# A memory of attention on one core: the segment's update ahead of its reads, the second half of the read and the update's addition a head later

## The chip, the cores and the metric

One Trainium2 chip; the program runs on one of its cores. The time is that of the device in microseconds (us), the median of several executions of the same program, lower is better. Engines are named as in the profile: PE is the matrix engine (PEld its weight loads), DVE the vector engine, ACT the scalar engine, POOL the GpSimd engine, SP the queue that issues the DMAs.

## The reference

A transformer block over 2048 tokens of width 1024, with 32 heads of 32. The first half is an attention that keeps a memory over four segments of 512 tokens, the second a token-mixing MLP. What matters here is the attention's loop over segments:

```python
phi = lambda t: jnp.where(t > 0, t + 1.0, jnp.exp(t))
for s in range(4):
    qs, ks, vs = q[:, :, s], k[:, :, s], v[:, :, s]
    p = softmax(qs @ ks.T * scale + mask)
    a_dot = p @ vs
    pq = phi(qs)
    a_mem = (pq @ M) / (pq @ z + 1e-6)
    outs.append(g * a_mem + (1 - g) * a_dot)
    pk = phi(ks)
    M = M + pk.T @ vs
    z = z + sum(pk)
```

A segment reads the memory (M, z) as the segments before it left it, and adds its own keys and values afterwards. M and z are zero in segment 0, and what segment 3 would add is read by nobody.

## The kernel before

The program has two parts. The attention (with the output projection's first products) fills the first 1045 us or so of the profile, the MLP the rest. The change lies in the attention alone.

**Tiles.** The 32 heads are taken in 8 groups of 4. A step t of the list `its` (32 of them) is one group and one segment: steps 0 to 15 go through the groups with segments 0 and 1, steps 16 to 31 through the groups again with segments 2 and 3. For each step `project(t, piece)` makes keys and values (pieces 0 and 1, 48 matmuls each, tile nps), queries (piece 2, 24 matmuls, tile qps, and the transposed keys, kps), the feature maps pq and pk, and in piece 3 the values' three bf16 parts and the step's work on the memory. For each of its 4 heads h, `maxima` computes scores a first time (sx, sy, sz) for the row maxima on DVE and turns them by a transpose (nmps) every second head; `scores` computes them again with the maxima as an extra row (a), exponentials on ACT, masks and low halves on POOL; `values` multiplies with the values (pv), and after the fourth head turns the result (ops).

**Order of the work.** One round of the main loop is one head: `scores(n)`, `maxima(n + 3)`, `values(n - 2)`, `project(n + 8)`. So the work on the memory of step t is written 8 heads ahead of that step's first scores. The rows of code only set priorities: a scheduler that knows the dependences reorders the instructions of every engine before the program is built. On the chip each engine then works through its own list strictly in order, and an instruction that waits holds up all behind it.

**The memory step** (`memory(t)`, lines 441 to 466). MZ holds M and z of all groups, 132 columns for each. In segments 1 to 3 the read is done in two halves (two of the segment's four tiles of 128 tokens in each): two matmuls pq by MZ into PSUM (rd, line 450), then three DVE instructions: add 1e-6 to the denominators (line 452), invert them (453), multiply (454, into am). In segments 0 to 2 four matmuls pk by v32 into PSUM follow (up, line 460). In segment 0 DVE writes them masked to MZ (462), in segments 1 and 2 to tm (465), which POOL adds to MZ (466). `am` is wanted by `values` of the same step, some six heads later.

**What they share.** rd, up, nmps, ops and two small transposes (mlt) all use the one PSUM bank with the tag "ms" (`bufs=1`): the next of them cannot start before DVE or ACT has read out the one before. v32, k32, pk and pq have one buffer each: the copies of the next step's values by ACT (line 399) wait until up has read v32.

**DVE's other work** on this stretch matters as well: the low halves of the weights that come in raw (line 122, wv and wq), and the reductions of the modulation's rows (line 573, rawm), which wait for a DMA of 512 KB each.

Of the kernel before, what the change touches and what calls it, by code (L numbers as in the profile page):

```python
# [7 lines left out]
F32 = mybir.dt.float32  # L8
# [4 lines left out]
ALU = mybir.AluOpType  # L13
# [5 lines left out]
P = 128  # L19
# [22 lines left out]
def attention_and_mlp(ctx, tc, x, wq, wkv, wo, beta, w1, b1, w2, b2, c, wm_a, wm_b, out):  # L42
    nc = tc.nc
    V, A, G, T, SY = nc.vector, nc.scalar, nc.gpsimd, nc.tensor, nc.sync
# [17 lines left out]
    a = par.__enter__()  # L62
# [9 lines left out]
    def bank(tag, bufs, name):  # L72
        return psum.tile([P, 512], F32, tag=tag, bufs=bufs, name=name)
# [36 lines left out]
    MZ = acst.tile([P, NG, 132], F32, name="MZ")  # L110
    bdg = acst.tile([P, NG, 132], F32, name="bdg")
# [73 lines left out]
    def kv_chunk(w, h, half, k, ps):  # L185
        wt = w["v", k // 2]
        o = 256 * (k % 2)
        n = 6 * k
        for i, j in ((0, 0), (0, 1), (1, 0)):
            for aa in range(2):  # L190
                tt = 2 * half + aa
                T.matmul(ps[:, aa], h[:, j, 128 * tt:128 * tt + 128], wt[:, i, o:o + 256],  # L192
                         start=(n == 0), stop=(n >= 6 * NK - 2), skip_group_check=True)
                n += 1
# [7 lines left out]
    def two_tiles(ps):  # L202
        return ps.rearrange("p (a n) -> p a n", a=2)
# [116 lines left out]
    for i in range(2):  # L320
        ps = bank("s2", 2, f"scps{i}")
# [22 lines left out]
    b = late.__enter__()  # L344
# [17 lines left out]
    its = [(pr, g, 2 * pr + i) for pr in range(2) for g in range(NG) for i in range(2)]  # L362
    NI = len(its)
    st = {}
# [13 lines left out]
    def project(t, piece):  # L378
        pr, g, seg = its[t]
        if piece == 0:  # L380
            st[t] = {}
        w = W[pr, g]
        hp = [hpages[seg, ct] for ct in range(NK)]
        d = st[t]
        if piece in (0, 1):
            if piece == 0:
                d["k32"] = pj.tile([P, 4, 128], F32, tag="k32", bufs=1, name=f"k32_{t}")
                d["v32"] = pj.tile([P, 4, 132], F32, tag="v32", bufs=1, name=f"v32_{t}")
                G.memset(d["v32"][:, :, 128:132], 1.0)
            half = piece  # L390
            k32, v32 = d["k32"], d["v32"]
            if t:
                ps = two_tiles(bank("pj", 2, f"nps{t}_{half}"))
                for k in range(NK):
                    kv_chunk(w, hp[k], half, k, ps)
            else:
                ps = two_tiles(first[half])
            A.copy(k32[:, 2 * half:2 * half + 2], ps[:, :, 0:128])
            A.copy(v32[:, 2 * half:2 * half + 2, 0:128], ps[:, :, 128:256])
        elif piece == 2:  # L400
            k32 = d["k32"]
            d["sg"] = sg = pj.tile([P, 4, L], F32R, tag="sg", bufs=1, name=f"sg{t}")
            ps = bank("pj", 2, f"kps{t}")
            for i in range(4):
                T.transpose(ps[:, 128 * i:128 * i + 128], k32[:, i], ident)
            split(sg[:, 2:4], ps, A, V)
            if t:
                ps = bank("pj", 2, f"qps{t}")
                for k in range(NK):
                    q_chunk(w, hp[k], k, ps)  # L410
            else:
                ps = first[2]
            split(sg[:, 0:2], ps, A, V)
            if seg:
                r = pj.tile([P, L], F32, tag="tmp", bufs=2, name=f"rq{t}")
                A.activation(r, ps, AF.Relu, scale=-1.0)
                A.activation(r, r, AF.Exp, scale=-1.0)
                d["pq"] = pj.tile([P, L], F32, tag="pq", bufs=1, name=f"pq{t}")
                V.scalar_tensor_tensor(d["pq"], ps, 0.0, r, op0=ALU.max, op1=ALU.add)
            if seg < 3:  # L420
                r = pj.tile([P, L], F32, tag="tmp", bufs=2, name=f"rk{t}")
                kf = k32.rearrange("p a n -> p (a n)")
                A.activation(r, kf, AF.Relu, scale=-1.0)
                A.activation(r, r, AF.Exp, scale=-1.0)
                d["pk"] = pj.tile([P, 4, 128], F32, tag="pk", bufs=1, name=f"pk{t}")
                V.scalar_tensor_tensor(d["pk"].rearrange("p a n -> p (a n)"), kf, 0.0, r, op0=ALU.max, op1=ALU.add)
            for h in range(3):
                stack(t, h)
        else:
            stack(t, 3)  # L430
            v = d["v32"][:, :, 0:128].rearrange("p a (h e) -> p a h e", h=4)
            vp = d["vp"] = b.tile([P, 4, 4, NV], BF16, tag="vp", bufs=3, name=f"vp{t}")
            r1 = pj.tile([P, 4, 4, 32], F32, tag="tmp", bufs=2, name=f"r1_{t}")
            G.memset(vp[:, :, :, 0:1], 1.0)
            A.copy(vp[:, :, :, 1:33], v)
            V.tensor_tensor(r1, v, vp[:, :, :, 1:33], op=ALU.subtract)
            A.copy(vp[:, :, :, 33:65], r1)
            V.tensor_tensor(vp[:, :, :, 65:97], r1, vp[:, :, :, 33:65], op=ALU.subtract)
            memory(t)

    def memory(t):
        pr, g, seg = its[t]
        d = st[t]
        d["am"] = am = b.tile([P, 4, 128], F32, tag="am", bufs=3, name=f"am{t}")
        if seg:
            for half in range(2):
                ps = bank("ms", 1, f"rd{t}_{half}")[:, 0:264].rearrange("p (a n) -> p a n", a=2)
                for aa in range(2):
                    i = 2 * half + aa
                    T.matmul(ps[:, aa], d["pq"][:, 128 * i:128 * i + 128], MZ[:, g], start=True, stop=True)  # L450
                rd = b.tile([P, 2, 4], F32, tag="rd", bufs=2, name=f"rdd{t}_{half}")
                V.tensor_scalar_add(rd, ps[:, :, 128:132], 1e-6)
                V.reciprocal(rd, rd)
                V.tensor_tensor(am[:, 2 * half:2 * half + 2].rearrange("p a (h e) -> p a h e", h=4),
                                ps[:, :, 0:128].rearrange("p a (h e) -> p a h e", h=4),
                                rd.unsqueeze(3).to_broadcast([P, 2, 4, 32]), op=ALU.mult)
        if seg < 3:
            ps = bank("ms", 1, f"up{t}")
            for i in range(4):
                T.matmul(ps[:, 0:132], d["pk"][:, i], d["v32"][:, i], start=(i == 0), stop=(i == 3))  # L460
            if seg == 0:
                V.tensor_tensor(MZ[:, g], ps[:, 0:132], bdg[:, g], op=ALU.mult)
            else:
                tm = b.tile([P, 132], F32, tag="tm", bufs=1, name=f"tm{t}")
                V.tensor_tensor(tm, ps[:, 0:132], bdg[:, g], op=ALU.mult)
                G.tensor_tensor(MZ[:, g], MZ[:, g], tm, op=ALU.add)

    def maxima(t, h):
        d = st[t]
# [123 lines left out]
    def at(f, n):  # L593
        if 0 <= n < 4 * NI:
            f(n // 4, n % 4)
# [3 lines left out]
    def seg_load(seg):  # L599
        seg_x[seg] = [load_x(s2p, tt) for tt in range(4 * seg, 4 * seg + 4)]  # L600
        return norm_all(seg_x[seg])
# [9 lines left out]
    with tc.issue_after(last_wm.ins):  # L611
        _, exp, _, normed_v = seg_load(1)
# [58 lines left out]
    for g in range(2, NG):  # L671
        n = 8 * g - 13
# [5 lines left out]
    for j in range(32):  # L678
        n = ML0 + 2 * j + (8 if j >= 8 else 0)
        later(n, lambda j=j: mod_fetch(j), n + (2 if j < 8 else 1), lambda r, j=j: mod_late(j, r), "V")  # L680
    plan(WO0 - 3, lambda: spread(gaw, 0))
    for i in range(8):
        n = WO0 + WOS * i
        later(n, lambda i=i: wo_fetch(i), n + 1, lambda r, i=i: wo_split(i, r), "G")

    for n in range(-LEADS, 4 * NI + VL):
        at(scores, n)
        at(maxima, n + LEADS)
        at(values, n - VL)
        m = n + LEADP  # L690
        if 0 <= m + 4 < 4 * NI:
            t = (m + 4) // 4
            if its[t][:2] not in W:
                with tc.issue_after(last_sk[t - 2 if t > 16 else 0, 3].ins):
                    load_w(its[t][1], its[t][0])
        if m >= 8:
            at(project, m)
        if 59 <= m < 67:
            seg, ct = 2 + (m - 59) // 4, 2 * ((m - 59) % 4)
            with ExitStack() as s:  # L700
                if seg == 3:
                    s.enter_context(tc.issue_after((last_sk[15, 3] if ct < 4 else last_nt[14, 3]).ins))
                reload_h(seg, ct)
                reload_h(seg, ct + 1)
        if 4 * NI - 5 <= m < 4 * NI + 3:
            i = m - 4 * NI + 5
            for c in (2 * (i % 4), 2 * (i % 4) + 1):
                wop[c, i // 4] = new_page(f"wo{c}_{i // 4}")
                if c < 5 or i < 4:
                    SY.dma_start(wop[c, i // 4].bitcast(F32), wos[c, i // 4])  # L710
        for f, engines in todo.pop(n, ()):
            with behind(n, engines):
                f()
# [135 lines left out]
    for products, tt in (((0, 1), 0), ((2,), 1), ((3, 4, 8), 8), ((9,), 9), ((10,), 2), ((11,), 10), ((12,), 3),  # L849
# [5 lines left out]
        for i in products:  # L855
            if i > 1:
                f = product(i)
# [283 lines left out]
```

## Time and profile before

| | |
|---|---|
| median of 3 executions | 2224.89 us (2224.09 to 2230.13) |
| the profiled execution: its own time / its span | 2226.6 us / 2224.9 us |
| PE busy in the span | 2190.3 us, 98% |
| DVE, ACT, POOL busy | 1666.7, 1135.7, 725.8 us |
| matmuls of the memory's reads (rd) / updates (up) | 192 records, 31.3 us / 192 records, 28.0 us |
| transposes of the maxima (nmps) in the same bank | 64 |

The matmuls of 32-bit data with 132 columns appear as two records each, so two rd matmuls are "x4" in a row of the timeline. Busy PE time in the profile contains modelled ends, so that neighbouring matmuls overlap; how many of one kind went through in a stretch of the timeline tells their rate better than the mean of one.

### The profile page before, as it was taken

What the parts mean: (1) busy time and instruction counts of PE and PEld (TensorE: products, weight loads), DVE (VectorE), ACT (ScalarE), POOL (GpSimd) and SP (SyncE); (2) the same over time, 40 slices, a digit from 0 to 9 for tenths busy, and PEclk for the clock granted to TensorE, in tenths of its full rate; (3) what the DMA queues carried; (4) which work ended last, traced back from release to release, by engine and by line L of the source; (5) the groups of instructions that cost most, each with busy time, mean ns of one, the idle gap of its engine ahead of it and who ended that gap; (6) DMA issues with size and microseconds to landing.
All of it is one profiled execution on the core that took longest, in us unless ns stands there. A gap on an engine that the chain in (4) does not pass through costs nothing.

```text
span 2224.9 us, 38052 instructions
## 1 busy us (share of the span) xinstructions
PE 2190.3 (98%) x13786; PEld 1881.0 (85%) x13786; DVE 1666.7 (75%) x3762; ACT 1135.7 (51%) x2050; POOL 725.8 (33%) x831
## 2 busy tenths in 40 slices
PE   8999999999999999999999999999999999999999
PEld 5988898888999999888888888888888888888887
DVE  7676777756777777664858766888888886969687
ACT  5486776756666666654636533533334242424232
POOL 2175766646767776663002200033330000000000
PEclk9999999999999999999999999999999999999999
DMA  7666666686556666664754687655556542414134
GB/s 287 192 187 191 175 181 193 189 279 216 170 180 205 188 183 211 193 219 143 231 194 186 226 304 275 243 223 220 204 202 219 206 148 64 145 57 147 57 123 151
DMA packets 175183, 423.03 MB, mean 190 GB/s; under 512 B 17524, under 2 KB 71828, under 8 KB 166036
## 3 DMA queue, kind: packets, MB, share of 16 engines
q1 hardware_dynamic: 174996, 420.61, 57.5%
q8 instruction: 109, 1.79, 0.3%
q14 instruction: 78, 0.64, 0.1%
HBM read 244.62 MB, written 125.06 MB: 166 GB/s over the span
## 4 chain that ended last, share of the span: by engine, by line
PE 87%; DVE 5%; DMA 3%; ACT 2%; POOL 1%; issue 1%; SPq 0%; DVEq 0%; ACTq 0%
PE mx L921 48%; PE nps L192 11%; PE po L791 8%; PE qps L200 7%; PE pv L544 3%; PE a L515 1%; PE sz L478 1%; PE sx L478 1%; DMA sk<-nt 1%; PE up L460 1%; PE a L518 1%; POOL p L530 1%; PE a L522 1%; PE sy L478 1%; PE rd L450 1%
## 5 line engine op out<-in xcount | busy, mean ns | idle before, releaser
L921 PE MATMUL mx<-bU,sp 128*128 128x512 f32 x2352 | 534.3, 389 | 0.9 <-DVE ac L928 0.9
L921 PEld LDWEIGHTS mx<-bU,sp 128*128 128x128 f32 x2352 | 441.3, 188 | 93.4 <-issue 1.3
L119 ACT CAST sp<-wr 128x384 fp32r<-128x384 f32 (+2 forms) x408 | 218.1, 547 | 431.8 <-PE mx L921 349.1
L192 PE MATMUL nps<-wv,h 128*128 128x256 f32 x3072 | 431.2, 283 | 1.6 <-DVE h L122 0.7
L921 PE MATMUL mx<-bA,sp 128*128 128x512 f32 x1764 | 430.5, 389 | 0.0
L530 POOL TENSOR_TENSOR p<-p,ph 128x640 f16<-128x640 f32 x256 | 380.2, 1485 | 138.5 <-ACT ph L528 134.5
L192 PEld LDWEIGHTS nps<-wv,h 128*128 128x128 f32 x3072 | 400.3, 189 | 9.4 <-DVE h L122 2.0
L921 PEld LDWEIGHTS mx<-bA,sp 128*128 128x128 f32 x1764 | 331.2, 188 | 68.7
L122 DVE TENSOR_TENSOR sp<-wr,sp 128x384 fp32r<-128x384 f32 (+2 forms) x408 | 259.8, 648 | 24.7 <-ACT sp L119 24.4
L928 DVE TENSOR_TENSOR ac<-mx,ac 128x512 f32<-128x512 f32 x280 | 189.9, 687 | 85.2 <-PE mx L921 84.1
L200 PE MATMUL qps<-h,wq 128*128 128x512 f32 x768 | 197.9, 400 | 0.0
L528 ACT CAST ph<-p 128x1280 f16<-128x1280 f32 x128 | 161.4, 1261 | 59.7 <-POOL p L526 59.6
L791 PE MATMUL po<-wo,ots 128*128 128x512 f32 x768 | 180.9, 391 | 0.0
L791 PEld LDWEIGHTS po<-wo,ots 128*128 128x128 f32 x768 | 142.7, 188 | 28.7
L200 PEld LDWEIGHTS qps<-h,wq 128*128 128x128 f32 x768 | 141.6, 190 | 27.7
L921 PE MATMUL mx<-bB,sp 128*128 128x512 f32 x588 | 164.0, 389 | 0.0
L526 POOL TENSOR_SCALAR_AFFINE_SELECT p<-p 128x256 f32<-128x256 f32 x256 | 134.1, 529 | 81.8 <-ACT p L523 53.9
L921 PEld LDWEIGHTS mx<-bB,sp 128*128 128x128 f32 x588 | 110.4, 188 | 22.9
L480 DVE CUSTOM_DVE_ANT_0 sz<-sz,mask 128x512 f32<-128x512 f32 x128 | 89.1, 696 | 52.0 <-PE sz L478 49.5
L480 DVE CUSTOM_DVE_ANT_0 sx<-sx,mask 128x128 f32<-128x128 f32 (+1 forms) x256 | 93.7, 366 | 44.1 <-PE sx L478 37.9
L928 DVE TENSOR_TENSOR cc<-mx,cc 128x512 f32<-128x512 f32 x140 | 94.9, 684 | 37.6 <-PE mx L921 37.4
L516 ACT ACTIVATE p<-a,shift 128x512 f32<-128x512 f32 x128 | 88.4, 691 | 41.2 <-PE a L515 40.4
(209 smaller groups left out, 3244.7 us busy)
## 6 DMA issues: line engine op xcount, KB each, us to landing
sk<-sg SPq DMA_DIRECT2D x384, 128.0 KB
wr<-in_w_dram SPq DMA_DIRECT2D x28, 1024.0 KB
wr<-in_w_dram SPq DMA_DIRECT2D x32, 768.0 KB
bstu<-ucd SPq DMA_DIRECT2D x28, 768.0 KB
wsp<-wv SPq DMA_DIRECT2D x32, 512.0 KB
rawm<-in_wm_b_dram SPq DMA_DIRECT2D x32, 512.0 KB
wv<-wsp SPq DMA_DIRECT2D x32, 512.0 KB
pcd<-cc SPq DMA_DIRECT2D x14, 1024.0 KB
```

The source lines that it names most:

```text
L119: last_hi[0] = A.copy(hi, src)
L122: return lo_eng.tensor_tensor(lo, src, hi.bitcast(F32), op=ALU.subtract)
L192: T.matmul(ps[:, aa], h[:, j, 128 * tt:128 * tt + 128], wt[:, i, o:o + 256], start=(n == 0), stop=(n >= 6 * NK - 2), skip_group_check=True)
L200: T.matmul(ps, wt[:, i, o:o + 128], h[:, j], start=(k + n == 0), stop=(3 * k + n == 3 * NK - 1))
L480: marks[4 * t + h - LEADS, "V"] = V.tensor_tensor_reduce(o, o, mask[:, 384 - 128 * i:], 1.0, -3.0e38, op0=ALU.add, op1=ALU.max, accum_out= ...
L516: A.activation(p32[:, 0:512], b0, AF.Exp, scale=SCALE, bias=shift)
L526: G.affine_select(w, w, pattern=[[0, 2], [1, 128]], compare_op=ALU.is_ge, fill=0.0, base=0, channel_multiplier=-1)
L528: marks[n, "A"] = A.copy(hi, p32)
L530: marks[n, "G"] = G.tensor_tensor(lo[:, c], p32[:, c], hi[:, c], op=ALU.subtract)
L791: T.matmul(ps, os_[:, i, P * ct:P * ct + P], wop[ct, nh][:, j], start=(n == 0), stop=(n == 3 * NK - 1))
L921: T.matmul(ps, ops[q][:, i, P * k:P * k + P], b[:, j], start=(m == 0 and first), stop=(m == 3 * nk - 1), skip_group_check=True)
L928: V.tensor_tensor(d, ps, d, op=ALU.add)
```

## The change

What was one call of `memory(t)` becomes two. Step 0, at the old place, first does the update (the four matmuls and DVE's masked copy), then the first half of the read. Step 1, called a head later in the main loop, behind piece 0 of the next step's `project`, does the second half of the read and POOL's addition of tm to MZ, which has to come behind both halves. In segment 0 nothing but the update is done, and MZ is written at once, as before. The instructions are the same in kind and number on every engine; pools and buffers are the same.

```diff
-            memory(t)
+            memory(t, 0)
...
-    def memory(t):
+    def read(t, half):
         pr, g, seg = its[t]
         d = st[t]
-        d["am"] = am = b.tile([P, 4, 128], F32, tag="am", bufs=3, name=f"am{t}")
-        if seg:
-            for half in range(2):
-                ps = bank("ms", 1, f"rd{t}_{half}")[:, 0:264].rearrange("p (a n) -> p a n", a=2)
...
+        ps = bank("ms", 1, f"rd{t}_{half}")[:, 0:264].rearrange("p (a n) -> p a n", a=2)
+        for aa in range(2):
+            i = 2 * half + aa
+            T.matmul(ps[:, aa], d["pq"][:, 128 * i:128 * i + 128], MZ[:, g], start=True, stop=True)
+        rd = b.tile([P, 2, 4], F32, tag="rd", bufs=2, name=f"rdd{t}_{half}")
+        V.tensor_scalar_add(rd, ps[:, :, 128:132], 1e-6)
+        V.reciprocal(rd, rd)
+        V.tensor_tensor(d["am"][:, 2 * half:2 * half + 2].rearrange("p a (h e) -> p a h e", h=4),
+                        ps[:, :, 0:128].rearrange("p a (h e) -> p a h e", h=4),
+                        rd.unsqueeze(3).to_broadcast([P, 2, 4, 32]), op=ALU.mult)
+
+    def update(t):
+        pr, g, seg = its[t]
+        d = st[t]
+        ps = bank("ms", 1, f"up{t}")
+        for i in range(4):
+            T.matmul(ps[:, 0:132], d["pk"][:, i], d["v32"][:, i], start=(i == 0), stop=(i == 3))
+        if seg == 0:
+            V.tensor_tensor(MZ[:, g], ps[:, 0:132], bdg[:, g], op=ALU.mult)
+        else:
+            d["tm"] = tm = b.tile([P, 132], F32, tag="tm", bufs=1, name=f"tm{t}")
+            V.tensor_tensor(tm, ps[:, 0:132], bdg[:, g], op=ALU.mult)
+
+    def memory(t, step):
+        pr, g, seg = its[t]
+        d = st[t]
+        if step == 0:
+            d["am"] = b.tile([P, 4, 128], F32, tag="am", bufs=3, name=f"am{t}")
+            if seg < 3:
+                update(t)
+            if seg:
+                read(t, 0)
+        elif seg:
+            read(t, 1)
+            if seg < 3:
+                G.tensor_tensor(MZ[:, g], MZ[:, g], d["tm"], op=ALU.add)
...
         if m >= 8:
             at(project, m)
+        if m % 4 == 0 and 0 < m <= 4 * NI:
+            memory(m // 4 - 1, 1)
```

Since the scheduler works on the whole attention, the order of all engines differs from step 1 on. Three places are shown, all of step 13 (group 6, segment 1). The first number in a name is the step: up13 is the update of step 13, rd13_1 the second half of its read, nps14 the next step's projection, nmps12_3 the transposed maxima of step 12; sy, sz and a are scores.

PE before, from the second half of the read to the update (pv matmuls and their weight loads stand where the dots are):

```order
L450 MATMUL rd13_1_6481<-MZ_127,pq13_6383 128x132 x2
...
L192 MATMUL nps14_0_6575<-wv0_7_1_1_6402,h0_7_451 128x256 x6
L192 MATMUL nps14_1_6692<-wv0_7_1_1_6402,h0_6_423 128x256 x5
L192 MATMUL nps14_1_6692<-wv0_7_1_1_6402,h0_7_451 128x256 x6
L478 MATMUL sy_13_1_6765<-sk1_1_502 128x384
L478 MATMUL sz_13_1_6768<-sk1_1_502 128x512
L521 MATMUL a2_12_0_6516<-sk0_0_497 128x128
L522 MATMUL a2_12_0_6516<-sk0_0_497 128x256
L515 MATMUL a0_12_1_6631<-sk0_1_498 128x512
L460 MATMUL up13_6488<-v32_13_6066,pk13_6388 128x132 x4
```

PE with the change, from the update to the first half of the read, and from there to the second half:

```order
L460 MATMUL up13_6474<-v32_13_6066,pk13_6388 128x132 x4
L493 MATMUL sz_13_1_6768<-sk1_1_502 128x512
L530 MATMUL a0_12_0_6502<-sk0_0_497 128x512
L533 MATMUL a1_12_0_6505<-sk0_0_497 128x384
L447 MATMUL rd13_0_6481<-MZ_127,pq13_6383 128x132 x2
...
L192 MATMUL nps14_0_6567<-wv0_7_1_0_6399,h0_4_367 128x256 x4
L192 MATMUL nps14_1_6692<-wv0_7_1_0_6399,h0_4_367 128x256 x4
L501 MATMUL nmps12_3_6528<-ident_90,mx12_2_6425 8x128
...
L493 MATMUL sy_13_2_6881<-sk1_2_503 128x384
L405 MATMUL kps14_6807<-ident_90,k32_14_6564 128x128 x2
L447 MATMUL rd13_1_6618<-MZ_127,pq13_6383 128x132 x2
```

The update stood behind the second half of the read and now stands ahead of the first. Between the two halves there is now a use of the bank by nmps12_3, and 40 nps matmuls lie between that and rd13_1.

DVE at the same place, before, from the end of the first half (am13 from rd13_0) to the end of the second:

```order
L454 TENSOR_TENSOR am13_6473<-rd13_0_6474,rdd13_0_6477 128x256
...
L573 SCALAR_TENSOR_TENSOR rawm5_6406,mcol_529<-rawm5_6406,scb_76 128x1024
L122 TENSOR_TENSOR wq0_7_0_0_6496<-rawq7_0_6279,wq0_7_0_0_6496 128x512
L122 TENSOR_TENSOR wq0_7_0_1_6499<-rawq7_0_6279,wq0_7_0_1_6499 128x512
L452 TENSOR_SCALAR rdd13_1_6484<-rd13_1_6481 128x8
L547 RECIPROCAL pv11_2_6546<-pv11_2_6546 128x4
L453 RECIPROCAL rdd13_1_6484<-rdd13_1_6484 128x8
L549 TENSOR_REDUCE red11_2_6568<-pv11_2_6546 128x128
L454 TENSOR_TENSOR am13_6473<-rd13_1_6481,rdd13_1_6484 128x256
```

and with the change:

```order
L465 TENSOR_TENSOR tm13_6479<-up13_6474,bdg_128 128x132
...
L449 TENSOR_SCALAR rdd13_0_6484<-rd13_0_6481 128x8
L450 RECIPROCAL rdd13_0_6484<-rdd13_0_6484 128x8
L451 TENSOR_TENSOR am13_6473<-rd13_0_6481,rdd13_0_6484 128x256
L122 TENSOR_TENSOR wv0_7_1_0_6399<-rawv7_1_6125,wv0_7_1_0_6399 128x512
L122 TENSOR_TENSOR wv0_7_1_1_6402<-rawv7_1_6125,wv0_7_1_1_6402 128x512
L588 SCALAR_TENSOR_TENSOR rawm5_6406,mcol_529<-rawm5_6406,scb_76 128x1024
L122 TENSOR_TENSOR wq0_7_0_0_6488<-rawq7_0_6279,wq0_7_0_0_6488 128x512
L122 TENSOR_TENSOR wq0_7_0_1_6491<-rawq7_0_6279,wq0_7_0_1_6491 128x512
L504 SCALAR_TENSOR_TENSOR nt1_12_3_6531<-nmps12_3_6528,nt0_12_3_6530 8x128
```

The reduction of rawm5 and the two weight splits behind it (wq) stood between the two halves of the read, on which the update waited. Now the update and the first half are read out ahead of them, the next step's weights (wv) come behind these, and what stands right behind rawm5 and wq is the reading out of nmps12_3.

More of the change, by code (lines that the diff above doesn't have):

```diff
@@ L438, in project @@
             V.tensor_tensor(vp[:, :, :, 65:97], r1, vp[:, :, :, 33:65], op=ALU.subtract)
-            memory(t)
-    def memory(t):
+            memory(t, 0)
+    def read(t, half):
         pr, g, seg = its[t]
         d = st[t]
-        d["am"] = am = b.tile([P, 4, 128], F32, tag="am", bufs=3, name=f"am{t}")
-        if seg:
-            for half in range(2):
-                ps = bank("ms", 1, f"rd{t}_{half}")[:, 0:264].rearrange("p (a n) -> p a n", a=2)
[L448 to L466, printed above, removed]
```

## The prediction

> **What bounds the kernel now.** I read the page first, then the busy time by stages, then what PE waited for in the stage that is changed, and last the timeline round its longest wait. The page, and the two stages:
>
> ```profile
> span 2224.9 us, 38052 instructions
> PE 2190.3 (98%) x13786; PEld 1881.0 (85%) x13786; DVE 1666.7 (75%) x3762; ACT 1135.7 (51%) x2050; POOL 725.8 (33%) x831
> ...
> 57.00:1045.00 988.00, 966.91 (x8348) 878.13 (x8347) 697.20 (x2065) 642.57 (x1146) 614.49 (x719) 0.99 0.65 194
> 1045.00:2225.00 1180.00, 1175.41 (x5183) 972.41 (x5181) 928.62 (x1614) 463.20 (x856) 99.15 (x64) 1.00 0.52 182
> ```
>
> (After the stretch and its length: PE, PEld, DVE, ACT, POOL busy, granted clock, DMA share, GB/s.) PE sets the time in both. The change touches the first stretch alone, in which PE is idle for 988.0 - 966.9 = 21 us of 988. The change leaves the number of matmuls as it is, so it can only alter these 21 us and the clock at which the rest runs. What PE waited for there (total, times, longest):
>
> ```profile
> PE a L515 <- DMA sk<-nt: 4.1, 5, 1.4
> PE up L460 <- DVE am L454: 3.8, 3, 3.5
> PE a L521 <- ACT p L516: 2.4, 3, 1.0
> ...
> PE sy L478 <- DVE rdd L453: 1.1, 1, 1.1
> ...
> PE kps L405 <- ACT v L399: 0.6, 1, 0.6
> ...
> PE nmps L486 <- DVE tm L465: 0.4, 1, 0.4
> ```
>
> The memory's own waits are few, but one of them, 3.5 us of up behind am, is the longest of the stretch. In PE's timeline (start, length, x number of records, idle time before it and what ended it):
>
> ```profile
> 438.63 2.91 PE L192 MATMUL nps<-wv,h 128*128 128x256 f32 x24
> 441.38 0.34 PE L478 MATMUL sy<-sk 96*128 96x384 f32 x1
> 441.56 0.40 PE L515 MATMUL a<-sk 98*128 98x512 f32 x1
> 441.79 0.34 PE L518 MATMUL a<-sk 98*128 98x384 f32 x1
> 441.97 0.62 PE L450 MATMUL rd<-MZ,pq 128*128 128x132 f32 x4
> 442.34 0.48 PE L478 MATMUL sz<-sk 96*128 96x512 f32 x1
> 442.65 0.61 PE L544 MATMUL pv<-vp,ph 128*128 128x97 bf16 x10
> 443.09 1.19 PE L192 MATMUL nps<-wv,h 128*128 128x256 f32 x8
> ...
> 448.13 0.70 PE L450 MATMUL rd<-MZ,pq 128*128 128x132 f32 x4
> ...
> 451.42 0.40 PE L515 MATMUL a<-sk 98*128 98x512 f32 x1
> 455.29 2.10 PE L460 MATMUL up<-v,pk 128*128 128x132 f32 x8 [3.48 <-DVE am L454]
> ```
>
> This is step 13. The second half of the read is issued at 448.13, PE works on until 451.8, and the update then waits 3.48 us for the bank. Why DVE was late, and what the granted clock did (eighth column of the windows):
>
> ```profile
> 449.51 1.92 DVE L573 SCALAR_TENSOR_TENSOR rawm<-rawm,scb 128x1024 f32<-128x1024 f32 x1 [1.55 <-DMA rawm<-in_wm_b_dram]
> ...
> 451.36 2.69 DVE L122 TENSOR_TENSOR wq<-rawq,wq 128x512 fp32r<-128x512 f32 x2
> 453.97 0.15 DVE L452 TENSOR_SCALAR rdd<-rd 128x8 f32<-128x8 f32 x1
> ...
> 454.73 0.41 DVE L454 TENSOR_TENSOR am<-rd,rdd 128x256 f32<-128x256 f32 x1
> ```
>
> ```profile
> 128.00:130.00 2.00, 1.35 (x7) 1.04 (x7) 1.95 (x9) 2.00 (x5) 2.00 (x5) 1.00 1.04 289
> 130.00:132.00 2.00, 1.45 (x8) 0.82 (x6) 1.74 (x6) 2.00 (x5) 0.71 (x3) 1.00 0.98 188
> ...
> 134.00:136.00 2.00, 2.00 (x13) 2.00 (x12) 2.00 (x2) 2.00 (x5) 1.92 (x2) 0.50 0.90 228
> ```
>
> ```profile
> 452.00:454.00 2.00, 0.00 (x0) 0.00 (x0) 2.00 (x3) 1.72 (x4) 1.51 (x2) 0.96 1.02 383
> 454.00:456.00 2.00, 0.71 (x3) 0.74 (x4) 2.00 (x10) 0.00 (x0) 0.52 (x2) 0.50 1.05 332
> ...
> 462.00:464.00 2.00, 2.00 (x6) 1.54 (x5) 2.00 (x8) 0.33 (x3) 1.14 (x2) 0.50 0.84 324
> 464.00:466.00 2.00, 2.00 (x10) 1.65 (x9) 1.69 (x3) 0.55 (x2) 1.96 (x2) 0.98 0.94 277
> ```
>
> DVE, in order, waited 1.55 us for rawm's DMA, reduced it, split two weights, and only then read out rd. PE's pause took the clock to half from 453.9 to 464.1, so the stall costs more than its own length.
>
> **The change part by part.** The sum is made against the profiled execution: its own time 2226.6 us (span 2224.9 and 1.7 round it), 1.7 us above the median of 2224.89.
>
> *The stall of step 13.* Now: 3.48 us idle, then 455.3 to 464.1 = 8.8 us at half clock, in which half as much gets done: 4.4 us more. Together 7.9 us. With the change the update stands ahead of the first half, and nothing waits for the second half's evacuation but the next user of the bank. What stands there instead is priced with these groups (count, then busy total, mean ns):
>
> ```profile
> L122 DVE TENSOR_TENSOR wv<-rawv,wv 128x512 fp32r<-128x512 f32 x27 | 36.0, 1358 | 3.5 <-ACT wv L119 3.5
> L454 DVE TENSOR_TENSOR am<-rd,rdd 128x256 f32<-128x256 f32 x48 | 20.2, 420 | 0.7
> L122 DVE TENSOR_TENSOR wq<-rawq,wq 128x512 fp32r<-128x512 f32 x14 | 18.1, 1306 | 0.4 <-ACT wq L119 0.3
> L489 DVE SCALAR_TENSOR_TENSOR nt<-nmps,nt 8x128 fp32r<-8x128 f32 x64 | 17.5, 274 | 19.5 <-ACT nt L488 19.4
> L453 DVE RECIPROCAL rdd<-rdd 128x8 f32<-128x8 f32 x48 | 9.4, 197 | 0.7
> L452 DVE TENSOR_SCALAR rdd<-rd 128x8 f32<-128x8 f32 x48 | 7.7, 160 | 14.7 <-PE rd L450 14.6
> ```
>
> First, the next step's nps needs the first wv split, which DVE now does behind the first half's evacuation: 0.16 + 0.20 + 0.42 + 1.36 = 2.1 us after rd. Beside it PE has ten pv matmuls (442.65 to 443.09: 0.45 us). That leaves a wait of about 1.6 us. Second, rd13_1 needs the bank that nmps12_3 holds until DVE's nt. DVE needs from the end of rd13_0: 0.8 for the evacuation, 2 x 1.36 (wv), 1.55 (rawm, by its usual length: 49.5 us for 32), 2 x 1.31 (wq), 0.27 (nt) = 8.0 us, and its wait for the DMA. That landed at 449.5, 6.9 us after rd13_0's end; since rd13_0 stands some 2.1 us of PE work later with the change (sz, two a and the four up among others), it lands 4.8 us after its end, DVE asks for it after 3.5, waits 1.3, and nt is done after 9.3 us. PE by then has 0.45 + 1.6 waited + 8 nps (0.9) + 40 nps at (441.38 - 438.63) / 24 = 0.115 us (4.6) + about 1.7 for ten pv, seven score and two kps matmuls at the spacings above = 9.3 us. So some 0.3 us of wait, if any. Left over: 1.9 us, in pieces of under 2 us. Term: **-7.9 + 1.9 = -6.0 us**. If the DMA is 2 us later than before, rd13_1 waits those 2 us as well; if the wv wait finds the score work already done, it is nothing: 0 to 4 us are left over.
>
> The clock could still fall. By the rows at 128 to 132, 1.2 us of idle time spread over 4 us was enough for the half clock at 134 (that spell lasted about 3.4 us by its three windows, 1.7 us lost). So a wait of 1.6 us may cost 1.7 more; this goes into the range, not into the sum.
>
> [...]
>
> *The other waits of the same kind.* The rest of up behind am (3.8 - 3.5 = 0.3 us), nmps behind tm (0.4; up and nmps stood next to each other in step 1), kps behind ACT's copy of v, which waits for up (0.6), and sy behind DVE's work on the denominators (1.1): all come from the two reads and the update following each other through one bank. With up first and the second half a head away they go: **-2.4 us**; bounds 0 and -2.4, and I take all, since in each of the 24 steps the update's own evacuation is one instruction of 0.3 us.
>
> *What is added.* The second half now stands between nmps of the odd heads and the next nmps or ops, in 24 places. Where that bank is tight, a wait of nmps's evacuation (ACT, then DVE's 0.27) or of rd's (0.78) falls on PE. Counting matmuls between two users of the bank at the spacings above, fewer than 2.2 us of PE work lie between them in 16 places with the change, 23 before. Below: nothing. Above: 24 x 0.78 = 18.7 us, if nothing covered them. The nearest rows are the short waits of today's chain, 0.3 + 0.4 us over 24 steps, so I take **+1.0 us**.
>
> POOL's addition of tm (16 instructions) is a head later; its result is read by the next segment's read, four heads or more on. pq is held a head longer, and is written again in the next piece 2, a head after the second half is due. v32, k32 and pk come free earlier. The DMAs are the same and SP is not asked for more. All that costs nothing unless DVE is late by a head, some 8 us.
>
> Sum: -6.0 - 2.4 + 1.0 = **-7.4 us**: 2219.2 for an execution like the profiled one, **2217.5 us** for the median.
>
> **The rivals.**
>
> *The stall moves instead of going.* rawm's DMA, the two wq splits and DVE's strict order are all still there. If the DMA lands 3 us later against PE, rd13_1 or pv catches the same 3.5 us and the half clock with it. For it: DMA is saturated there (shares of 1.02 and 1.05). Against it: the 9.3 us of work that now stand between. Then only the small waits change: 2224.9 - 2.4 + 1.0 = 2223.5 us. A new cold spell anywhere else in the reordered attention gives about the same, 2217.5 + 7.9 = 2225.4.
>
> *Slower: the bank becomes a chain through the maxima.* nmps, then rd's second half, then the next nmps or ops: each waits for DVE's evacuation of the last, and nt feeds the DMA on which the second score pass waits already (4.1 us, 5 times). It decides where DVE needs longer than PE has work in between, about 3.4 us. Then step 13, where DVE is latest, is held up as it is today and keeps its 7.9 us; if half of the 24 second halves lose their 0.78 us, that is 9.4 us, and one more spell at half clock adds 4.4: 2224.9 - 2.4 + 9.4 + 4.4 = 2236 us. For it: the bank has its 170 uses as before, and one of them now waits between two evacuations that feed the maxima. Against it: DVE is busy for 697 of 988 us and has time to catch up.
>
> *Nothing happens,* because the scheduler would put the pieces back where they were: the orders of PE and DVE exclude it.
>
> **How the numbers follow.** 0.3%, 6.7 us, is about what a measurement of this kernel can tell from no change. The forecast has 0.50, and since its -7.4 lies close to that bound and its left-over wait is 0 to 4 us, 0.40 of this is faster and 0.10 the same. The stall that moves has 0.27: 0.22 same, 0.02 faster, 0.03 slower. The slower chain has 0.23: 0.22 slower, 0.01 same. Together: faster 0.42, same 0.33, slower 0.25. The forecast's own range is 2211 to 2222: downward nothing left over, nothing added and the cold spell at 134 gone as well (2217.5 - 1.9 - 1.0 - 1.7 = 2213) and 2 us of the 11 us of other idle time; upward 4 us left over, half of the small waits still there, and 1.7 us of half clock (2217.5 + 2.1 + 1.2 + 1.7). The whole range takes in the stall that moves and reaches almost to the slower case's 2236; below, it allows for half of the idle time that is left of the 21 us: 2208 to 2235.
>
> **What would show it.** In the profile of the changed kernel: up waits for am nowhere; no window near 450 to 465 with a clock of 0.5; PE's idle time between 57 and 1045 falls from 21 to about 13 us, with a wait of 1 to 2 us of nps behind wv in step 13, and rd behind nt at 0.3 us; ACT's copies of v no longer wait for up. Wrong would be the forecast if that stall or a half clock shows at another instruction (the first rival), or if rd behind nt and nmps or ops behind am sum up to 8 us or more (the second).

## The result, and the profile after

| kernel | median of its runs, us | lowest to highest | ratio to before (95% interval) |
| --- | --- | --- | --- |
| before | 2225.33 (6 runs) | 2223.67 to 2230.13 | |
| with the change | 2239.56 (6 runs) | 2237.44 to 2241.12 | 1.0060 (1.0047 to 1.0073) |

The change makes the kernel 14.2 us (0.6%) slower. 2217.5 was forecast, and the range ended at 2235.

The head of the page of the changed kernel, and then its two stages (after the stretch and its length: PE, PEld, DVE, ACT, POOL busy, granted clock, DMA share, GB/s):

```profile
span 2238.5 us, 38027 instructions
PE 2196.8 (98%) x13786; PEld 1884.4 (84%) x13786; DVE 1666.9 (74%) x3762; ACT 1135.1 (51%) x2050; POOL 722.1 (32%) x831
```

```profile
57.00:1045.00 988.00, 962.21 (x8310) 873.14 (x8309) 692.90 (x2060) 642.94 (x1145) 611.01 (x719) 0.99 0.64 193
1045.00:2238.00 1193.00, 1186.22 (x5225) 980.19 (x5223) 933.59 (x1620) 462.71 (x858) 98.96 (x64) 1.00 0.52 181
```

In the attention PE's idle time did not fall from 21 us to 13; it rose to 988.0 - 962.2 = 25.8 us. At the end of that stretch 8348 matmuls were through before, 8310 now, and the rest has to be done later.

From 1045 us on, PE's list is the same in both kernels. The first matmul of this common part starts 9.5 us later with the change, the last one 13.4 us later. So 3.9 us of the loss arise in the second stretch, which the change does not touch. PE's waits after 1150 us, first before, then with the change:

```profile
PE mx L921 <- DVE ac L928: 0.9, 1, 0.9
```

```profile
PE mx L938 <- DVE ac L945: 2.6, 2, 1.7
PE mx L938 <- ACT sp L119: 1.1, 2, 0.7
```

That is 2.8 us more of idle time. Over the kernels of this study the idle time behind 1045 us lies between 0.9 and 3.7 us; whether the 3.7 belong to the change's order or to this one execution is not shown.

**The place that was forecast** looks much as forecast. PE's timeline in step 13 (start, length, instruction, x records, idle time before it and what ended it):

```profile
449.72 0.45 PE L493 MATMUL sy<-sk 96*128 96x384 f32 x1 [0.42 <-DVE mx L495]
...
450.24 1.06 PE L460 MATMUL up<-v,pk 128*128 128x132 f32 x8
451.05 0.48 PE L493 MATMUL sz<-sk 96*128 96x512 f32 x1
452.22 0.47 PE L530 MATMUL a<-sk 98*128 98x512 f32 x1 [0.69 <-ACT ph L543]
...
452.71 0.61 PE L447 MATMUL rd<-MZ,pq 128*128 128x132 f32 x4
...
455.75 0.96 PE L192 MATMUL nps<-wv,h 128*128 128x256 f32 x6 [0.87 <-DVE wv L122]
```

The update runs ahead of the read and waits for nothing, where it had waited 3.48 us. The spell at half clock (granted 0.50) from 453.8 to 464.1 is gone. The wait of nps for the wv split is there, 0.87 us where 1.6 was forecast.

**What took its place** stands elsewhere. What PE waited for in the attention now (total, times, longest):

```profile
PE nps L192 <- DVE sg L122: 2.6, 1, 2.6
PE a L536 <- ACT p L531: 2.6, 4, 1.2
PE a L530 <- DMA sk<-nt: 2.4, 4, 1.4
PE nps L192 <- DVE wv L122: 2.0, 3, 0.9
PE nps L192 <- ACT wv L119: 1.9, 2, 1.3
PE pv L559 <- DVE red L566: 1.9, 3, 1.0
PE sx L493 <- DMA sk<-sg: 1.9, 2, 1.7
PE sz L493 <- DVE mx L495: 1.5, 3, 1.0
...
PE up L460 <- DVE pk L426: 1.3, 1, 1.3
PE kps L405 <- ACT k L398: 1.1, 1, 1.1
...
PE rd L447 <- DVE tm L465: 0.7, 1, 0.7
```

Most of them do not belong to the memory: they are projections waiting for weights or for the step before, and scores and values waiting for maxima, exponentials and transposed maxima. The memory's own are up behind pk, which is the very first update (at 60 us) and waited 1.3 us before the change too, and the last row. And the half clock (0.50) stands at three places where it did not stand before, from 334.0, 433.0 and 497.8 us on. The second, in windows of two us:

```profile
428.00:430.00 2.00, 0.63 (x17) 0.51 (x14) 2.00 (x4) 1.83 (x3) 1.89 (x2) 1.00 0.00 0
430.00:432.00 2.00, 1.34 (x5) 0.71 (x5) 1.93 (x7) 1.41 (x3) 2.00 (x2) 1.00 0.00 0
432.00:434.00 2.00, 0.88 (x3) 0.48 (x3) 2.00 (x10) 1.48 (x2) 0.63 (x3) 0.75 0.89 186
434.00:436.00 2.00, 1.65 (x9) 1.45 (x10) 1.74 (x4) 2.00 (x5) 1.92 (x2) 0.50 0.92 197
```

PE was idle for 3.15 of the 6 us from 428 to 434, in short pieces, with DVE at work for 5.9 us of that time. The clock fell to 0.50 at 433.0, when 2.2 us of this had gone by. The third place is the longest wait of the stretch; the timelines of PE, ACT and SP's queue there, and the windows behind it:

```profile
498.45 2.93 PE L192 MATMUL nps<-wv,h 128*128 128x256 f32 x12 [2.56 <-DVE sg L122]
```

```profile
497.09 0.58 ACT L119 CAST sg<-kps 128x512 fp32r<-128x512 f32 x1 [6.19 <-DMA sk<-nt]
```

```profile
468.80 6.81 SPq L359 DMA_DIRECT2D h<-hT  x8
476.56 0.68 SPq L374 DMA_DIRECT2D sk<-sg  x1
...
492.50 0.58 SPq L376 DMA_DIRECT2D sk<-sg  x1
```

```profile
498.00:500.00 2.00, 1.55 (x7) 1.55 (x8) 2.00 (x8) 1.21 (x3) 0.41 (x1) 0.50 0.38 111
500.00:502.00 2.00, 2.00 (x11) 1.90 (x10) 0.26 (x2) 1.23 (x2) 0.00 (x0) 0.50 1.01 387
502.00:504.00 2.00, 2.00 (x11) 1.90 (x10) 1.93 (x8) 0.00 (x0) 0.00 (x0) 0.50 0.83 248
```

Read backwards: nps waits for DVE's low half of the transposed keys (sg), DVE for ACT's cast, ACT stood 6.2 us waiting for a transfer of sk, and SP's queue sent eight reloads of the activations (h<-hT, 6.8 us) ahead of this step's first sk. A run below holds the reloads back. Nothing of this is part of the memory step; it is where the reordered attention happens to be at that moment.

**The account of the time.** From the traces of all 18 kernels of this study: PE's idle time ahead of matmuls after 57 us, plus what the clock lost (length of each spell times one minus the granted clock), and the rest of the profiled execution's time.

| kernel | profiled, us | idle | lost to the clock | rest |
| --- | --- | --- | --- | --- |
| before | 2226.6 | 22.0 | 6.8 | 2197.8 |
| with the change | 2240.6 | 29.5 | 8.5 | 2202.6 |
| fastest of the study | 2216.6 | 16.3 | 0.0 | 2200.3 |
| slowest of the study | 2242.9 | 33.2 | 6.8 | 2202.9 |
| all 18 | 2216.6 to 2242.9 | 16.3 to 33.2 | 0 to 10.2 | 2196.1 to 2203.6, mean 2200.8 |

So idle time and half clock account for most of what sets these kernels apart: 24 us between the fastest and the slowest of 26. For the change they are 7.5 + 1.7 = 9.2 us of the profiled difference of 14.0; of the 7.5, 4.7 lie in the attention and 2.8 behind it. Some 0.4 us were lost ahead of the 57 us from which the table counts, where the changed kernel has one more spell, of 3.4 us at 50.7 us. For the remaining time the trace shows no wait of PE; it is within the 7.5 us by which the rest scatters over the kernels.

The table has one execution of each kernel, and the spells are not the same in every execution. PE's list is the same in all 18 kernels up to 82 us, and yet three of them have a spell at 50.3 to 50.7 us and fifteen have none. On one chip 21 executions of the kernel before had granted clocks of 0.995 to 0.999 over the whole span; one of 0.995 took 2233.9 us, the one of 0.999 took 2224.3 us. So what an order costs in half clock is partly chance.

### The profile page after: what moved, and what is told of

Same layout as the page of the kernel before. It is cut to its first block, busy times and chain, and to the rows that moved or that the text cites. A ratio compares the mean times of both kernels' runs of the same rounds, so it can differ in the third digit from the quotient of the medians.

```text
span 2238.5 us, 38027 instructions
## 1 busy us (share of the span) xinstructions
PE 2196.8 (98%) x13786; PEld 1884.4 (84%) x13786; DVE 1666.9 (74%) x3762; ACT 1135.1 (51%) x2050; POOL 722.1 (32%) x831
## 4 chain that ended last, share of the span: by engine, by line
PE 87%; DVE 4%; DMA 4%; ACT 2%; POOL 1%; issue 1%; SPq 0%; ACTq 0%; DVEq 0%
PE mx L938 46%; PE nps L192 13%; PE qps L200 7%; PE po L808 7%; PE pv L559 4%; PE a L530 1%; PE sz L493 1%; PE sx L493 1%; POOL p L545 1%; PE a L533 1%; PE sy L493 1%; PE rd L447 1%; PE up L460 1%; PE a L537 1%; DMA sk<-sg 1%
## 5 line engine op out<-in xcount | busy, mean ns | idle before, releaser
L538 ACT ACTIVATE p<-a,shift 128x384 f32<-128x384 f32 x128 | 74.2, 580 | 66.3 <-PE a L537 65.5
```

## The experiments

Four theories run through the expectations. A: the change makes a new order of the whole attention, and that order happens to put other waits and half clock in PE's way. B: the second half, a head late, makes the chain through the one bank longer. C: the update ahead of the read costs. D, formed after the first runs: the two parts of the change cost together. Times in one row come from one chip.

### One part alone, one half of the steps alone

The change has two parts, the update first and the second half a head late. Against the changed kernel:

```diff
+        first, late = True, False     # e1: update first, nothing late
+        # e2: False, True    e3: t >= 16, t >= 16    e4: t < 16, t < 16
...
-            if seg < 3:
+            if first and seg < 3:
                 update(t)
             if seg:
                 read(t, 0)
-        elif seg:
+                if not late:
+                    read(t, 1)
+            if not first and seg < 3:
+                update(t)
+        elif seg and late:
             read(t, 1)
-            if seg < 3:
-                G.tensor_tensor(MZ[:, g], MZ[:, g], d["tm"], op=ALU.add)
+        if seg in (1, 2) and step == late:
+            G.tensor_tensor(MZ[:, g], MZ[:, g], d["tm"], op=ALU.add)
```

> One part of the change alone: the update ahead of the reads, both halves of the read and POOL's addition behind it at the old place. Theory A (the loss of 14.2 us is made by the new order of the whole attention, which puts other waits and half-clock spells in PE's way; the memory step itself costs nothing): the order of every engine is drawn anew here too, so the time is neither that of before nor that of the change but somewhere from 2220 to 2240 us, and the two parts alone do not add up to +14. Theory B (the second half, a head later, lengthens the chain through the bank): the late half is not here, so 2225 us within 3 us. Theory C (the update ahead of the reads costs): 2239 us within 3 us.

> The other part alone: first half of the read, then the update at the old place, second half and addition a head later. Theory A: somewhere from 2220 to 2240 us, its difference from before plus that of the update-first kernel not 14 us. Theory B: 2239 us within 3 us, with rd behind nt, or nmps and ops behind am, as new waits of PE that sum up to 5 us or more. Theory C: 2225 us within 3 us.

> The whole change, but only for steps 16 to 31 (segments 2 and 3); up to some 480 us the program is that of before. Theory A: no share of the loss belongs to it by itself; since the spells at half clock and the waits that were worst in the change lie before 510 us, 2220 to 2230 us. Theory B or C: 16 of the 24 changed reads and 8 of the 16 changed updates are here, so half to two thirds of the loss, 2232 to 2235 us.

> The whole change for steps 0 to 15 alone (segments 0 and 1); up to some 480 us the program is that of the change. Theory A: the attention is 5 to 7 us behind that of before at 510 us, as the change was, and what comes behind is drawn anew, 2228 to 2240 us. Theory B or C: a third to a half of the loss, 2230 to 2232 us, spread evenly over the steps and not at two or three places.

| run | median, us | before on that chip | difference |
| --- | --- | --- | --- |
| e1 update first | 2231.59 | 2227.98 | +3.6 |
| e2 half late | 2215.85 | 2227.98 | -12.1 (ratio 0.9936, 0.9920 to 0.9953) |
| e3 second pass | 2234.01 | 2227.98 | +6.0 |
| e4 first pass | 2235.64 | 2227.98 | +7.7 |

The two halves of the steps add up to the change (13.7 of 14.2). For e3 theory A had expected 2220 to 2230 us and failed, while the 2232 to 2235 of B and C held; for e4 A's range held and theirs failed. The traces show why the sum need not speak against A: up to 543 us PE's list in e4 is that of the change, and from 640 us on PE's list in e3 is that of the change, so each has the change's own order in its half.

The two parts do not add up: 3.6 - 12.1 = -8.5 against +14.2. The late half makes the chain through the bank longer, and is the fastest kernel of the study, below the one before; so that chain (theory B) is not what costs. Its attention:

```profile
57.00:1045.00 988.00, 974.83 (x8413) 887.07 (x8411) 704.69 (x2084) 646.82 (x1154) 613.03 (x719) 1.00 0.65 197
```

Its idle time is 988.0 - 974.8 = 13.2 us, which is what had been forecast for the whole change, and the profiled execution has no spell of half clock in the attention.

### The wait at 498 taken away

```diff
+                if seg == 2:
+                    s.enter_context(tc.issue_after(last_sk[14, 3].ins))
```

The reload of the activations of segment 2 is held until step 14's last sk has been sent.

> The changed kernel, with the reload of segment 2's normed tokens held back until the last head rows of step 14 are issued; up to some 465 us the program is that of the change. In the change SP issues six reloads in a row (469.9 to 475.6 us) ahead of step 14's head rows, ACT then waits 6.2 us for their landing before it may overwrite sg, PE waits 2.6 us at 498 us, and 6.8 us at half clock follow. If that is what this place costs: the wait and the spell at 498 us are gone, 2.6 + 3.4 = 6 us, so the attention is that much less behind at 510 us. Theory A (order of the whole): what follows is drawn anew, so the end is 2 to 10 us under the change. Theory D (the two parts of the change together cost by themselves): no more than the 6 us, and the loss behind 510 us (3 us in the attention) stays as it is.

Measured 2237.55 us, 9.4 us above the kernel before on that chip (2228.1), where the change has 14.2. The wait of nps for sg is gone, and the first rows of PE's waits are now:

```profile
PE a L533 <- DMA sk<-nt: 8.0, 4, 3.5
PE sx L496 <- DMA sk<-sg: 3.4, 3, 1.4
```

The transposed maxima come late instead (8.0 us where the change has 2.4). One wait taken away by a new order of the queue came back as another: the attention's idle time is 26.4 us, where the change has 25.8, and in place of the spell at 497.8 there is one of the same 6.8 us at 521.2.

### The same order drawn anew: token tiles shifted

The token tiles (one DVE job every six heads) have nothing to do with the memory. Put one or two heads later, they make the scheduler reorder nearly the whole attention again (PE's list differs from 89 us on), under each of the memory's versions:

```diff
-        later(6 * i, lambda i=i: load_gaw(i),
-              6 * i + 3, lambda r, i=i: token_tile(8 + i), "V")
+        later(6 * i + 1, lambda i=i: load_gaw(i),
+              6 * i + 4, lambda r, i=i: token_tile(8 + i), "V")
```

(With 2 and 5 for two heads.)

> A control: the kernel before with other work, the normalizing of segment 2's and 3's tokens, written one head later; the memory is untouched, but the order of all engines differs from step 2 on. Theory A: as much of a new draw as the change was, so the time moves by 3 to 15 us either way against before. Theory D: within 3 us of before.

> The same shift on the changed kernel. Theory A: its distance to the control made from before is not the 14 us of the change, but differs from it by 5 us or more. Theory D: 14 us above that control, within 4 us.

> The same shift on the kernel with the second half late and the update at its old place (12 us under before without the shift). Theory A: the gain shrinks or goes, its distance to the control made from before is anywhere from -10 to +10 us. Theory D: 12 us under that control, within 4 us.

> The kernel before with its token tiles two heads later; the memory step is as before. A third draw of the control, after 2228.1 (no shift) and 2233.7 (one head). Theory A (what decides is where the new order of the whole attention happens to let TensorE wait and fall to half clock): somewhere between 2222 and 2240. Theory D (the two parts of the change together cost by themselves): the same, since D says nothing of the control; D speaks of the distances to it in the other three.

> The whole change with the token tiles two heads later. So far it stood 14 us above its control without a shift and 9 us above it with one head of shift. D: again 8 to 14 us above h1. A: the distance to h1 is drawn anew, between -6 and +12 us, and a value under +4 would speak for A.

> The second half of the read and the addition a head later, the update at its old place; token tiles two heads later. So far 12 us and 6.5 us below its control. D: 5 to 12 us below h1. A: between -12 and +6 us of h1; above -2 would speak for A.

> The update ahead of both halves of the read, nothing a head later; token tiles two heads later. Without a shift it stood 3 us above its control. D: 0 to 5 us above h1, since only the two parts together cost. A: anywhere between -6 and +10 us. If h2 and h4 both lie well above h1, and h3 below, it is the update's place ahead of the read that costs, whatever the second half does (theory C).

| shift | control | the change | half late alone | update first alone |
| --- | --- | --- | --- | --- |
| none | 2225.33 / 2227.98 | +14.2 | -12.1 | +3.6 |
| one head | 2233.72 (before 2228.1) | 2242.89, +9.2 | 2227.23, -6.5 | not run |
| two heads | 2229.52 (before 2227.61) | 2236.81, +7.3 | 2224.10, -5.4 | 2235.31, +5.8 |

("Control" is the kernel before with the same shift; the differences are those to it.) A shift that computes nothing new moves the kernel before by 5.6 and by 1.9 us. The first is nearly as large as the gain of 7.4 that was forecast. With one head, theory D's three bounds failed: the control within 3 us, the change 10 to 18 us above it (missed by 0.8), the late half 8 to 16 us below it; A's held, that for the change barely. Yet in three draws of three the change is above its control and the late half alone below it. With two heads D's bounds for the change (8 to 14) and for the update alone (0 to 5) were missed by under 1 us, while the value under +4 that would have spoken for A did not come: this spoke for something systematic. With two heads the change and the update alone lie well above the control and the late half below it; that was the sign, named beforehand, that the update's place ahead of the read costs (theory C). The draws are not quite independent: PE's list in the change with a shift of one head is the same as without it from about 645 us on.

### Is it the read right behind the update?

In the changed kernel DVE waits longer for the read than with the late half alone. DVE's groups for the first instruction of the evacuation, first of the change, then of the late half alone (count, busy, mean ns, idle before it and what ended it):

```profile
L449 DVE TENSOR_SCALAR rdd<-rd 128x8 f32<-128x8 f32 x48 | 7.8, 162 | 23.8 <-PE rd L447 22.8 <-PE pv L559 0.8
```

```profile
L449 DVE TENSOR_SCALAR rdd<-rd 128x8 f32<-128x8 f32 x48 | 7.6, 158 | 6.0 <-PE rd L447 5.9
```

The second longest one of the change, on DVE:

```profile
944.29 0.35 DVE L566 SCALAR_TENSOR_TENSOR red<-red,gate,pv 128x128 f32<-128x128 f32 x1
947.24 0.17 DVE L449 TENSOR_SCALAR rdd<-rd 128x8 f32<-128x8 f32 x1 [2.61 <-PE rd L447]
947.36 0.30 DVE L495 CUSTOM_DVE_ANT_0 sx<-sx,mask 128x128 f32<-128x128 f32 x1
```

DVE stood 2.6 us before the read's denominators, with work on maxima behind it. Theory C, sharpened, made of this a cause: with the update first, the read waits in the one bank for the update's evacuation, DVE waits for the read, and maxima come late to PE. Four kernels move the pieces apart or together (in the notation "step | a head later"; u update, 0 and 1 the halves, + the addition; the change is u 0 | 1 +):

```diff
 # i1: u | 0 1 +        i4: the same, token tiles one head later
 # i2: 0 | u 1 +
 # i3: 0 | 1 u +
 # (in segment 0, where nothing is read, i2 and i3 leave the update at its step)
```

> The update at its old step, both halves of the read and the addition a head later, so that no read stands right behind an update. Theory C (a read right behind the update in the one bank costs: it cannot start before the update is evicted, VectorE has the read's eviction next in its order and waits for it, 22.8 us in all in the change, 5.9 us with the second half late alone, and maxima and value tiles behind it come late): VectorE's wait for rd under 12 us, TensorE's waits in scores and values back from 11.9 to about 5 to 7 us, time 2216 to 2228. Theory D (update ahead and late half together cost wherever they stand): 2235 to 2242. Theory A (scatter of a new order): 2216 to 2240, without a tie to VectorE's wait for rd.

> The first half of the read at its old step; the update, then the second half right behind it, and the addition a head later. C: a read stands right behind an update again, so VectorE waits for rd 15 us or more, scores and values idle 9 us or more, time 2232 to 2242. D: the first half is read before the update, as with the late half alone: 2214 to 2226. A: 2216 to 2240 without a tie to VectorE's wait.

> As the run before, but with the second half of the read ahead of the update: no read stands right behind an update. C: VectorE waits for rd under 10 us, time 2214 to 2226, at least 8 us below the run before. D: the same time as the run before within 4 us. A: 2216 to 2240, no order between the two.

> The first of these four with the token tiles one head later, where the control stood at 2233.7 and the change at 2242.9. C: VectorE's wait for rd under 12 us and the time at or below the control, 2224 to 2234. D: 2240 to 2246. A: 2222 to 2244.

| run | median, us | against before (2230.49) | DVE's wait for rd | a read right behind an update |
| --- | --- | --- | --- | --- |
| i1 | 2223.85 | -6.6 | 16.7 | no |
| i2 | 2236.89 | +6.4 | 5.6 | yes |
| i3 | 2237.88 | +7.4 | 20.8 | no |
| i4 | 2238.83 | +8.3 | 17.3 | no |

The same group of DVE, of i2 and of i3:

```profile
L449 DVE TENSOR_SCALAR rdd<-rd 128x8 f32<-128x8 f32 x48 | 7.7, 161 | 6.1 <-PE rd L447 5.6
```

```profile
L449 DVE TENSOR_SCALAR rdd<-rd 128x8 f32<-128x8 f32 x48 | 7.7, 160 | 21.0 <-PE rd L447 20.8
```

The cause that theory C had been given falls. Its bounds for DVE's wait failed in all four runs, though its ranges for the time held in i1 and i2. i2 and i3 take the same time with 5.6 and 20.8 us of that wait, and i1 is fast with 16.7. i4 is i1 with the token tiles shifted, and the two lie 15 us apart, where the control moved by 5.6. Theory D, that update first and late half cost together wherever they stand, expected i1 at 2235 or more and falls with it. D expected i2 at 2214 to 2226, too, and it took 2236.9; only its equal times for i2 and i3 came. Only theory A's ranges held all four. They were so wide that this proves little by itself, and i2 and i3 are one order each, where i1 and i4 show how far two orders can lie apart; but A is what is left.

## Why the prediction was wrong

**The stall of step 13, term -6.0: right.** The 3.48 us wait and its half clock are gone. Of the 1.9 us to be left over, 0.87 us is there (nps behind wv), and rd behind nt does not wait at all. The row of rawm's DMA, on which the first rival stood, caught nothing else in that place. The 4.4 us of clock in this term are those of one execution: one that ran at 0.999 over 2224 us lost at most 3.3 us to the clock in all (the granted clock is on record to three digits).

**The other small waits, term -2.4: right.** None of the four rows (up behind am, nmps behind tm, kps behind v, sy behind the denominators) appears in the list of the changed kernel.

**What is added, +1.0: right in size.** The memory's own new wait is rd behind tm, 0.7 us. The slower rival, whose 2236 us came closest to the result, had the wrong mechanism: by its own test, rd behind nt and nmps or ops behind am of 8 us or more, it did not happen. They sum to 0.1 us.

**ACT's copies of v, which were to wait for up no longer: wrong.** They waited 9.2 us before and 5.8 us after, both times in 7 places.

**The sum: this step failed.** "Sum: -6.0 - 2.4 + 1.0" adds the memory's own waits and holds all others at their old value. Before, those others were 21.1 - 3.8 - 1.1 - 0.6 - 0.4 = 15.2 us of the attention's idle time. After, they are 25.8 - 0.7 - 0.9 = 24.2 us: 9 us more, more than the whole gain forecast. The half clock, of which 10.2 us of 13.7 were to go, is 17.1 us, in three new spells. And where the rival that moves the stall spoke of "a new cold spell anywhere else in the reordered attention", it put one such spell at 7.9 us; the sign it gave, a half clock at another instruction, came true three times over, and the new waits beside it had no price. The prediction also held that only the first stretch could alter, and 2.8 us of new idle time stand in the second. Moving some ten instructions in each step made the scheduler rewrite the lists of the engines through the whole attention, and the waits of 1 to 3 us that this puts in new places were not priced. Shifts of the token tiles alone show the size of that term: +5.6 and +1.9 us.

**What stays open.** That 9.2 of the 14.0 us are PE's idle time and half clock, nearly all outside the memory step, is shown by the rows and the account above; the other 4.8 us are not traced to a wait of PE. Which relation of the change makes it come out above its control three times of three is not shown either. The longer chain through the bank alone does not cost, the reload at 498 is not most of it, and DVE's wait for the read does not go with the time. The update ahead of the read, alone, gave 3.6 of the 14.2 us in one order and 5.8 of the 7.3 in another, so it may be a part of the cause. Three draws of one sign happen by chance one time in four, so a plain unlucky order isn't excluded.

## What to carry to other kernels

Where a scheduler rewrites the lists of all engines, a forecast made from the waits at the changed place alone is the smaller half: price the reordering as well, by a neutral change of order that costs two runs, and take a gain under that scatter (here some 6 us of 2225) as unproven until a second draw shows it. Try the parts of a change apart; here the late half alone took 2215.85 us, and stayed 5 to 12 us below its control in three orders, while the two parts together lost. When the bound engine is 98% busy, compare kernels by its idle time plus what the clock lost: this account told more than any single wait.

## What the hardware showed that was not expected

All spells of half clock before the last matmul, in all 18 kernels, are 3.41 us long or two or three times that. Before, they are 3.4 and 10.2 us long and start at 133.0 and 453.8. With the change they are 3.4, 3.4, 6.8 and 6.8 us long and start at 50.7, 334.0, 433.0 and 497.8. In all six of these the granted clock is 0.50. The distance between the two starts before is 94 times 3.413 us, those between the starts with the change are 83, 29 and 19 times that, and in every other trace with several spells they are whole multiples too, to 0.01 us: in these traces the clock fell on a grid of that step. The spell at 433 began after idle time in pieces, not after one idle stretch: in the 3.41 us ahead of it PE was idle for 1.2 us, for 0.6 us at most at a time. It lasted until 439.8, though PE was idle for only 0.35 of the 5.8 us from 434 on. Over all traces, PE was idle for 0.8 to 3.4 us in the step of the grid ahead of a spell (46 spells, 25 of them with less than 1.9 us); ahead of the six spells named here it was 0.8 to 2.0 us. Among the steps of the attention that no spell followed (in the 17 traces whose spells show the grid), none has more than 1.9 us; before and with the change none has more than 1.5. Between 0.8 and 1.9 us both occur, and the traces do not tell what decides.

So the loss came in steps of up to 1.7 us: half of 3.41, by the granted 0.50. The waits ahead of 433.0 were followed by 6.8 us at half clock, 3.4 us lost; the 13.2 us of idle time in the attention of the kernel with the late half alone were followed by none in its profiled execution.
